# One row of the second MLP matrix in four loads on 16, 5, 11 and 3 DMA engines

## The chip, the cores and the metric

The kernel runs on one core of a Trainium2 chip: TensorE (PE), VectorE (DVE), ScalarE (ACT), GpSimd (POOL) and SyncE (SP), each with its own instruction stream, and 16 DMA engines that move data between HBM and the on-chip memory (128 partitions). The metric is the device time of one execution in microseconds, as the median of several runs. Before the change it is 364.54 us (3 runs, 364.46 to 364.63).

## The reference

One decode step: attention over the last 2048 positions of a key and value cache, an MLP on the same input rows, and a gate that mixes the two. All data are bfloat16.

```python
B, Sq, D = 8, 1, 576;  Hq, Hkv, Sk, Dh = 32, 16, 8192, 128      # MLP: F = 4608
g = sigmoid((x * gate_w).sum(-1))
q = (x @ wq) per head
a = softmax(q @ k[last 2048].T * Dh**-0.5) @ v[last 2048] @ wo
y = layernorm(x);  b = gelu(y @ w1 + b1) @ w2 + b2
out = g * a + (1 - g) * b
```

The cache parts that are read are 2 x 64 MB; `w2`, the second MLP matrix, has 4608 x 576 elements (5.3 MB).

## The kernel before

**How it is built.** `build_kernel` describes every operation as an `_Op` with its engine, the operations it waits for (`deps`), those it only has to stand behind (`after`), and a cost. `_Plan.schedule` (L62) runs a list schedule over these costs, which gives the order on each engine; `_Plan.emit` (L141) writes each engine's stream in that order, with semaphore waits for the `deps`. All loads are issued by SP on one hardware queue, and each one has the one before it in `after` (`last_dma`), so that their order is that in which the code makes them. A load raises its semaphore by 16 in all.

**Where the data lie.** All buffers are views of one tensor, `arena`; `req` reserves space, `over` lays a view over another one. `RAW` holds four slots of 32 KB a partition and a smaller fifth. `take_slot` goes round the four; a load into a slot waits for the slot's readers (`slot_free`). The views `sel` (L254) and `sel4` (L255) hold 0/1 matrices that PE reads once, near the start, in `sel_pe` (`o_selp`) and `h_pe` (`o_hp`).

**The stages.** At the start the query, the gate, and the hidden layer of the MLP are computed; `hT` holds the hidden layer transposed, 36 row groups of 128 rows (`FT = 36`). Then 16 units of attention (`NU`), each with a 4 MB K load and a 4 MB V load: VectorE transposes K, PE makes the scores, VectorE and ScalarE the softmax, PE the product with V. The list `stream` gives the order of the loads: K and V interleaved with K ahead, then at the end `("M", 0), ("W", 0), ("W", 1), ("M", 1)` (L594).

**The end.** `M` is a part of the second MLP matrix, `W` half of the attention's output matrix (`wo_chunk`, L832). Partition p of `w2` holds the rows 36 p to 36 p + 35, so that one "row" of the code is 576 elements (1152 B) in each of the 128 partitions. `M_CUTS` (L593) cuts the 36 into loads: `[24]` for the first part, `[8, 3, 1]` for the second. `m2_chunk` (L858) issues these loads, each with a semaphore of its own (`t0` to `t3`), and for each of them makes groups of matmuls: for every row two (288 columns each) that add `hT[:, row] x w2 row` into one PSUM bank. `AccGroup` (L570) is such a group; all groups of the end add into the same bank (`BK_ACC`), in the order of the list `o_m2`. When the last is done, VectorE and ScalarE copy the two halves out (L896 to L902), and SP stores the result (L903).

The lines that the change and the prediction speak of: the load of K and V (L618), the loads of the output matrix (L836), the loads of `w2` (L865), the matmuls of an `AccGroup` (L579), the product with V (L755, and its loop L188).

Of the kernel before, what the change touches and what calls it, by code (L numbers as in the profile page):

```python
# [6 lines left out]
BF = mybir.dt.bfloat16  # L7
F32 = mybir.dt.float32
ACTF = mybir.ActivationFunctionType
ALU = mybir.AluOpType  # L10
# [28 lines left out]
class _Plan:  # L39
# [10 lines left out]
    def add(self, eng, fn, deps=(), name=None, cost=0.1, after=(), prio=0):  # L50
        op = _Op(eng, fn, deps, name, cost, after=after, prio=prio)
        op.idx = len(self.all)
        self.all.append(op)
        return op

    def dma(self, eng, fn, semkey, nbytes, deps=(), name=None, after=(), prio=0):
        op = _Op(eng, fn, deps, name, self.DMA_ISSUE, after=after, is_dma=True, dma_sem=semkey, nbytes=nbytes, prio=prio)
        op.idx = len(self.all)
        self.all.append(op)
        return op  # L60
# [106 lines left out]
def _pst(t):  # L167
    return t.ap().ap[0][0]
# [23 lines left out]
        tile_size=(128, 128), tile_position=(0, 0)))  # L192


def build_kernel(nc, A_x, A_k_cache, A_v_cache, A_wq, A_wo, B_x, B_w1, B_b1, B_w2, B_b2, gate_w, out):
    B, Sq, D = A_x.shape
    _, Hkv, Sk, Dh = A_k_cache.shape
# [2 lines left out]
    W = min(4096, max(256, Sk // 4))  # L200
# [8 lines left out]
    ND = 4  # L209
    SE = 4 * W  # L210
    DE = 2 * SE
    FC, FT = 4, 36
# [12 lines left out]
    with ExitStack() as es:  # L225
        R = {}
        aoff = [0]

        def req(name, nelem, dt, align=64):
            sz = 2 if dt == BF else 4  # L230
            o = aoff[0] + ARENA_BASE
            o = (o + align - 1) // align * align - ARENA_BASE
            R[name] = (o, nelem, dt)
            aoff[0] = o + nelem * sz

        def over(name, base, off, nelem, dt):
            R[name] = (R[base][0] + off, nelem, dt)
            assert off + nelem * (2 if dt == BF else 4) <= R[base][1] * (2 if R[base][2] == BF else 4)
# [12 lines left out]
        req("idf8", 8, F32)  # L251
        req("dg", 16, F32)
        req("ones8", 128, F32)
        req("sel", 4 * 128, BF)  # L254
        req("sel4", 128, BF)  # L255
        req("cols", 16, F32)
        req("xT", 6 * 32, BF)
        req("yT", 6 * 32, BF)
# [17 lines left out]
        req("KT", 2 * SE // 2, BF)  # L276
        req("RAW", ND * DE + WOR * D, BF, 512)
        over("maskR", "PC", 0, 512, BF)
        over("out_sb", "PC", 1024, D, BF)
        over("KT2", "RAW", 2 * ND * DE, SE, BF)  # L280
        over("x_sb", "BD", 0, D, BF)
# [14 lines left out]
        arena = es.enter_context(nc.sbuf_tensor("arena", [128, (aoff[0] + 1) // 2], BF))  # L296
        AST = _pst(arena)
        arena_f = arena.bitcast(F32)

        def aoffs(name):  # L300
            return R[name][0] // 2
# [4 lines left out]
        def view(name, parts=128):  # L306
            o, n, dt = R[name]
            a = arena[0:parts, o // 2: o // 2 + (n * (2 if dt == BF else 4)) // 2]
            if dt == F32:
                a = a.bitcast(F32)  # L310
            return a
# [8 lines left out]
        sel = view("sel").rearrange("p (c m) -> p c m", c=4)  # L320
# [4 lines left out]
        sel4 = view("sel4", FC)  # L325
# [6 lines left out]
        hT = view("hT").rearrange("p (t b) -> p t b", b=32)  # L332
# [19 lines left out]
        def slot(s):  # L352
            return RAW[:, s * DE:min((s + 1) * DE, ND * DE + WOR * D)]
# [8 lines left out]
        def col(i, parts=128):  # L362
# [10 lines left out]
        OC = 64  # L373

        eng_sems = {e: es.enter_context(nc.semaphore("sem_" + e)) for e in ENGS}
        dma_keys = ["x", "g", "b", "b2", "wq", "w1", "out"] + ["s%d" % i for i in range(ND + 1)] + ["t%d" % i for i in range(5)]
        dma_sems = {k: es.enter_context(nc.semaphore("dma_" + k)) for k in dma_keys}

        P = _Plan()
        add, dma = P.add, P.dma  # L380
# [7 lines left out]
                   deps=[o_idf], name="r8", cost=0.2)  # L388
# [141 lines left out]
        o_selp = add("pe", sel_fn, deps=[o_qt, o_sel, o_xg], name="sel_pe", cost=0.9, prio=9)  # L530
# [20 lines left out]
        o_hp = add("pe", h_fn, deps=dw1 + db + [o_yT, o_xT, o_gcol, o_homg, o_sel4, o_obl], name="h_pe", cost=5.0)  # L551
# [10 lines left out]
        o_hT = add("dve", lambda e: e.transpose(view("hT"), bass.AP(arena, offset=aoffs("hb"), ap=[[AST, 128], [1, FT], [FT, 32]])), deps=[o_hf], name="hT", cost=1.3)  # L562
# [23 lines left out]
        NU = NG * NT  # L586
        stream, nk = [], 0
        for vi in range(NU):
# [1 line left out]
                stream.append(("K", nk))  # L590
                nk += 1
            stream.append(("V", vi))
        M_CUTS = [[24], [8, 3, 1]]  # L593
        stream += [("M", 0), ("W", 0), ("W", 1), ("M", 1)]  # L594

        last_dma = [d_w1r]
# [9 lines left out]
        def take_slot():  # L606
            n = n_slot[0]
            n_slot[0] += 1
            return (1, 2, 0, 3)[n % ND]
# [13 lines left out]
        def query(g):  # L623
            qb_done[g] = []
            for a in range(4):
                def fn(e, a=a):
                    dst = bass.AP(arena, offset=32 * a * AST + aoffs("qbd") + 640 * (g % 2) + 32 * a + 16, ap=[[AST, 32], [160, 4], [1, 16]])
                    src = bass.AP(arena, offset=32 * a * AST + aoffs("q4") + 32 * (NB_ * g + a // 2) + 16 * (a % 2), ap=[[AST, 32], [256, 4], [1, 16]])
                    return e.tensor_copy(dst, src)  # L629
                qb_done[g].append(add("pool", fn, deps=o_q4 + [o_qz, qk_unit.get(NT * (g - 1) - 1)], name="qr%d_%d" % (g, a), cost=0.3))  # L630
# [213 lines left out]
        o_m2, o_bias = [], []  # L844
# [10 lines left out]
        def bias(i):  # L855
            o_bias.append(AccGroup("m2_b", [(ob[:, 0:8], b2_sb), (ob[:, 8:16], b2_sb)], [d_b2, o_obl, o_obh], cost=0.6, after=[o_hp]).op)

        def m2_chunk(ci):  # L858
            s = take_slot()
            j = sum(sum(c) for c in M_CUTS[:ci])  # L860
            at = 0
            src = B_w2.rearrange("(p j) n -> p (j n)", j=FT)
            ops = []
            for n, jn in enumerate(M_CUTS[ci]):
                d = dma("sp", (lambda j=j, jn=jn, at=at: lambda e: e.dma_start(slot(s)[:, at * D:(at + jn) * D], src[:, j * D:(j + jn) * D]))(),  # L865
                        "t%d" % (sum(len(c) for c in M_CUTS[:ci]) + n), 128 * jn * D * 2, deps=slot_free[s] if n == 0 else [], name="d_w2_%d_%d" % (ci, n), after=last_dma[-1:])
                last_dma.append(d)
                mms = [(hT[:, j + k, 0:8], slot(s)[:, (at + k) * D:(at + k + 1) * D]) for k in range(jn)]
                for q in range(0, jn, 8):
                    ops.append(AccGroup("m2_%d_%d_%d" % (ci, n, q), mms[q:q + 8], [o_hT, d], cost=0.14 * min(8, jn - q), prio=-1 if ci == 0 else 0, after=o_m2[-1:]).op)  # L870
                    o_m2.append(ops[-1])
                j, at = j + jn, at + jn
            slot_free[s] = ops

        query(0)
        bias(0)
        for kind, i in stream:
            {"K": k_item, "V": v_item, "W": wo_chunk, "M": m2_chunk, "B": bias}[kind](i)

        seq = []  # L880
        for t in range(NU):
# [31 lines left out]
def bass_gated_mix__sliding_block_cached__mixer_channel_mlp__decode_kernel(  # L913
    nc: bass.Bass,
    A_x: bass.AP,
    A_k_cache: bass.AP,
    A_v_cache: bass.AP,
    A_wq: bass.AP,
    A_wo: bass.AP,
    B_x: bass.AP,  # L920
    B_w1: bass.AP,
    B_b1: bass.AP,
    B_w2: bass.AP,
    B_b2: bass.AP,
    gate_w: bass.AP,
    out: bass.AP,
):
    build_kernel(nc, A_x, A_k_cache, A_v_cache, A_wq, A_wo, B_x, B_w1, B_b1, B_w2, B_b2, gate_w, out)
# [28 lines left out]
```

## Time and profile before

| | |
|---|---|
| median of 3 runs | 364.54 us |
| span of the profiled execution, first to last instruction | 363.0 us |
| busy: PE, VectorE, ScalarE, GpSimd | 297.9, 231.4, 168.6, 22.9 us |
| DMA queue of the loads | 6092 packets, 154.30 MB |
| landing of the last three loads after their issue | 22.3 to 23.0 us |

The profile is of one execution. Its page gives busy time by engine, the span in 40 slices (a digit is the busy share in tenths), the DMA queues, and the chain of work that ended last. The timeline lists instructions as start, duration, engine, line, operation, target and source and count, with the idle time before them and what ended it in brackets. A window's row gives its length, the busy time of each engine with its number of instructions, then three columns: granted TensorE clock, mean busy share of the 16 DMA engines, and GB/s. PEld is PE's weight load, SPq the issue of a load by SP. A packet counts into the window in which it starts, so that a share can be a little over 1.

### The profile page before, as it was taken

How to read it: one execution, taken by the hardware profiler on the slowest of the kernel's cores; microseconds unless marked ns; L12 is line 12 of the kernel's file. 1: busy time of each engine (PE TensorE's matmuls, PEld its weight loads, DVE VectorE, ACT ScalarE, POOL GpSimd, SP SyncE). 2: the span in 40 equal slices, each digit the busy share in tenths (PEclk: the TensorE clock that was granted, in tenths of full speed). 3: DMA queues.
4: the chain of work that ended last, by engine and by line, in shares of the span. 5: the costliest groups of instructions: out<-in, count | busy, mean ns of one | idle time of the engine just before them, and what ended most of it. 6: DMA issues, size and time to landing. Idle time of an engine off the chain costs nothing.

```text
span 363.0 us, 4821 instructions
## 1 busy us (share of the span) xinstructions
PE 297.9 (82%) x1954; PEld 125.3 (35%) x1423; DVE 231.4 (64%) x166; ACT 168.6 (46%) x130; POOL 22.9 (6%) x52
## 2 busy tenths in 40 slices
PE   0456366999999979998897979997989698999875
PEld 0111000434252615242433417150615152436742
DVE  0452989576666694929385768566675949295720
ACT  1022106656647463663637373838374554656000
POOL 9032030000010000000100000000000000003000
PEclk9976598999999998999999989999999999999999
DMA  8999999999999999999999999999999999999996
GB/s 347 436 437 406 455 412 455 412 455 412 450 415 451 415 451 413 441 426 441 426 441 426 435 430 437 430 437 428 437 430 437 430 435 430 437 430 433 415 430 257
DMA packets 6102, 154.45 MB, mean 426 GB/s; under 512 B 694, under 2 KB 840, under 8 KB 1228
## 3 DMA queue, kind: packets, MB, share of 16 engines
q1 hardware_dynamic: 6092, 154.30, 98.8%
q8 instruction: 8, 0.13, 0.1%
q14 instruction: 2, 0.02, 0.0%
HBM read 154.29 MB, written 0.01 MB: 425 GB/s over the span
## 4 chain that ended last, share of the span: by engine, by line
DMA 56%; DVE 27%; PE 14%; issue 1%; ACT 1%; SPq 0%; POOL 0%
DMA arena<-in_A_k_cache_dram 47%; DVE arena L718 21%; PE ps L175 6%; DMA arena<-in_B_w_dram 6%; DMA arena<-in_A_x_dram 3%; DVE arena L668 2%; PE ps L188 2%; PE ps L755 2%; PE ps L732 2%; DVE arena L645 1%; PE ps L501 0%; PE ps L579 0%; DVE arena L557 0%; DVE arena L521 0%; ACT arena L536 0%
## 5 line engine op out<-in xcount | busy, mean ns | idle before, releaser
L718 DVE STREAM_TRANSPOSE arena<-arena 128x4096 f32<-128x4096 f32 (+1 forms) x34 | 141.7, 4175 | 21.9 <-DMA arena<-in_A_k_cache_dram 21.9
L674 ACT ACTIVATE arena<-arena 32x2048 bf16<-32x2048 bf16 x60 | 114.5, 1908 | 71.4 <-DVE arena L668 42.9
L175 PE MATMUL ps<-arena 128*128 128x512 bf16 (+3 forms) x531 | 136.1, 402 | 0.0
L188 PE MATMUL ps<-arena 128*128 x840 | 109.5, 277 | 7.3 <-issue 1.2
L188 PEld LDWEIGHTS ps<-arena 128*128 x840 | 81.4, 97 | 34.3 <-issue 19.0
L732 PE MATMUL ps<-arena 128*128 128x512 bf16 x128 | 51.4, 401 | 27.6 <-DVE arena L718 26.1
L645 DVE TENSOR_REDUCE arena<-ps 128x1 f32<-128x2048 f32 x16 | 36.7, 2291 | 53.8 <-PE ps L175 53.8
L732 PEld LDWEIGHTS ps<-arena 128*128 128x128 bf16 x128 | 12.5, 98 | 131.7 <-issue 75.3
L649 ACT ACTIVATE arena<-ps,arena 128x2048 bf16<-128x2048 f32 x16 | 40.7, 2543 | 0.5
L646 ACT ACTIVATE arena<-arena 128x1 f32<-128x1 f32 x16 | 3.2, 203 | 63.5 <-DVE arena L645 63.5
L755 PE MATMUL ps<-arena 128*128 128x256 bf16 x184 | 25.3, 272 | 1.1 <-DVE arena L663 1.1
L755 PEld LDWEIGHTS ps<-arena 128*128 128x128 bf16 x184 | 16.9, 99 | 18.8 <-issue 14.6
L668 DVE STREAM_TRANSPOSE arena<-arena 128x1024 f32<-128x1024 f32 x15 | 18.1, 1205 | 2.9 <-ACT arena L649 2.9
L579 PE MATMUL ps<-arena 128*8 128x288 bf16 (+1 forms) x140 | 9.6, 286 | 4.0 <-DMA arena<-in_A_wo_dram 3.3
L739 POOL MEMSET arena<- 128x4096 f32 x1 | 3.5, 3511 | 148.2 <-PE ps L175 148.2
L685 PE MATMUL ps<-arena 128*128 128x512 bf16 x16 | 6.5, 407 | 6.5 <-ACT arena L649 5.2
L629 POOL COPY arena<-arena 32x64 bf16<-32x64 bf16 x16 | 3.7, 229 | 123.3 <-PE ps L175 122.4
L901 ACT ACTIVATE arena<-ps 8x288 bf16<-8x288 f32 x1 | 0.4, 402 | 19.5 <-PE ps L579 19.5
L422 DVE COPY arena<-arena 8x128 bf16<-8x128 bf16 x2 | 0.5, 228 | 13.9 <-DMA arena<-in_A_x_dram 13.9
L579 PEld LDWEIGHTS ps<-arena 128*8 128x8 bf16 (+1 forms) x140 | 5.8, 86 | 9.9 <-DMA arena<-in_A_wo_dram 3.3
L900 DVE CAST arena<-ps 8x288 bf16<-8x288 f32 x1 | 0.4, 446 | 12.3 <-PE ps L579 12.3
L557 DVE TENSOR_TENSOR arena<-arena 128x1152 f32<-128x1152 f32 x1 | 1.4, 1358 | 9.7 <-ACT arena L555 9.7
(106 smaller groups left out, 94.0 us busy)
## 6 DMA issues: line engine op xcount, KB each, us to landing
arena<-in_A_k_cache_dram SPq DMA_DIRECT2D x16, 4096.0 KB, 28.7
arena<-in_A_v_cache_dram SPq DMA_DIRECT2D x16, 4096.0 KB, 25.5
arena<-in_B_w_dram SPq DMA_DIRECT2D x1, 4608.0 KB, 22.0
arena<-in_A_wo_dram SPq DMA_DIRECT2D x2, 2304.0 KB, 23.8
arena<-in_A_wq_dram SPq DMA_DIRECT2D x1, 4096.0 KB, 12.6
arena<-in_B_w_dram SPq DMA_DIRECT2D x1, 3456.0 KB, 24.1
arena<-in_B_w_dram SPq DMA_DIRECT2D x1, 1152.0 KB, 22.3
arena<-in_B_w_dram SPq DMA_DIRECT2D x1, 576.0 KB, 23.0
```

Source lines behind the costliest of these rows:

```text
L175: return e.add_instruction(mybir.InstMatmult(name=nc.get_next_instruction_name(), engine=mybir.EngineType.PE, ins=[e.lower_ap(rhs), e.lowe ...
L188: return e.add_instruction(mybir.InstMatmult(name=nc.get_next_instruction_name(), engine=mybir.EngineType.PE, ins=[rhs, lhsT], outs=[e.low ...
L579: ins = e.matmul(ps[32 * j:32 * j + 8, BK_ACC, 0:JN], lhsT, rhs[:, JN * j:JN * j + JN], start=False, stop=True, skip_group_check=True, til ...
L629: return e.tensor_copy(dst, src)
L645: mx = add("dve", lambda e: e.tensor_reduce(out=k(g, MX + x), in_=scores, axis=AXL.X, op=ALU.max), deps=[qk_unit[t]], name="mx%d" % t, cos ...
L649: ex = add("act", lambda e: e.activation(out=bass.AP(arena, offset=aoffs("P"), ap=[[AST, 128], [64, 32], [1, 2], [2, 32]]), in_=ps[:, 0:4, ...
L668: pc = add("dve", lambda e: e.transpose(view("PC").bitcast(F32), view("P").bitcast(F32)), deps=[ex] + (sp_done[t - 1][0] if t else [o_acc0 ...
L674: return e.activation(out=bass.AP(arena, offset=32 * a * AST + aoffs(home) + 64 * a, ap=[[AST, 32], [256, 32], [1, 64]]), in_=bass.AP(aren ...
L685: mm = e.matmul(*args, start=True, stop=False, skip_group_check=True) if n == 0 else held_matmul(nc, e, *args, start=True, stop=False, ski ...
L718: return e.transpose(bass.AP(arena_f, offset=foffs(base) + 2048 * h0, ap=[[AST // 2, 128], [1, 2048 * nh]]), bass.AP(arena_f, offset=foffs ...
L732: mm = e.matmul(*args, start=False, stop=True, skip_group_check=True) if rc == 0 else held_matmul(nc, e, *args, stop=True, skip=True)
L755: return e.matmul(dst, bass.AP(arena, offset=aoffs(home) + 256 * q + ee, ap=[[AST, 128], [2, 128]]), slot(s).rearrange("p (r k d) -> p r k ...
```

## The change

The last row (row 35) of each partition's part of `w2` leaves the 8-row load, which becomes one of 7 rows, and comes in four loads of its own, made by `row_part`. `X_PARTS` gives for each of them a number of DMA engines and of partitions on each: 16 x 1, 5 x 14, 11 x 3 and 3 x 3, which are 128 in all. The source of each load has the engines' number as its outermost dimension; `grouped_read` hands both patterns to the DMA instruction as they are. The four stand in `stream` behind the last V load and between the loads M0, W0, W1 and M1. They share one semaphore (`w2x`); the row's two matmuls (`m2_x`) wait for the last of the four and stand behind the second output-matrix group, ahead of the 7-row group. The row lies in a view `w2x` over the space of `sel` and `sel4`, and the first load waits for these views' readers.

```diff
+def grouped_read(nc, e, dst, src):
+    return e.add_instruction(mybir.InstDMACopy(
+        name=nc.get_next_instruction_name(), engine=mybir.EngineType.SP, queue="qSPDynamicHW", mode="Copy",
+        ins=e.lower_ap_dma(src), outs=e.lower_ap_dma(dst), oob_is_err=True, cce_op=ALU.bypass))
...
-        req("sel", 4 * 128, BF)
-        req("sel4", 128, BF)
+        req("selb", 5 * 128, BF)
...
+        over("sel", "selb", 0, 4 * 128, BF)
+        over("sel4", "selb", 1024, 128, BF)
+        over("w2x", "selb", 0, D, BF)
...
-        M_CUTS = [[24], [8, 3, 1]]
+        M_CUTS = [[24], [7, 3, 1]]
...
+            if ci == 1:
+                o_m2.append(AccGroup("m2_x", [(hT[:, FT - 1, 0:8], w2x)], [o_hT, d_w2x[-1]], cost=0.2, prio=-1, after=o_m2[-1:]).op)
...
+        w2x = view("w2x")
+        X_PARTS = [(16, 1), (5, 14), (11, 3), (3, 3)]
+        d_w2x = []
+
+        def row_part(i):
+            n, m = X_PARTS[i]
+            p0 = sum(a * b for a, b in X_PARTS[:i])
+            dst = bass.AP(arena, offset=p0 * AST + aoffs("w2x"), ap=[[AST, n * m], [1, 1], [1, D]])
+            src = B_w2.rearrange("(p j) n -> p (j n)", j=FT)[p0:p0 + n * m, (FT - 1) * D:FT * D].rearrange("(n m) c -> n m c", n=n)
+            d_w2x.append(dma("sp", lambda e: grouped_read(nc, e, dst, src), "w2x", n * m * D * 2, deps=[o_selp, o_hp] if i == 0 else [], name="d_w2x%d" % i, after=last_dma[-1:]))
+            last_dma.append(d_w2x[-1])
+
+        stream = stream[:2 * NU] + [("R", 0), ("M", 0), ("R", 1), ("W", 0), ("R", 2), ("W", 1), ("R", 3), ("M", 1)]
```

More of the change, by code (lines that the diff above doesn't have):

```diff
@@ L375, in build_kernel @@
         eng_sems = {e: es.enter_context(nc.semaphore("sem_" + e)) for e in ENGS}
-        dma_keys = ["x", "g", "b", "b2", "wq", "w1", "out"] + ["s%d" % i for i in range(ND + 1)] + ["t%d" % i for i in range(5)]
+        dma_keys = ["x", "g", "b", "b2", "wq", "w1", "w2x", "out"] + ["s%d" % i for i in range(ND + 1)] + ["t%d" % i for i in range(5)]
         dma_sems = {k: es.enter_context(nc.semaphore("dma_" + k)) for k in dma_keys}
@@ L873, in m2_chunk @@
             slot_free[s] = ops
+        w2x = view("w2x")
[8 more added lines that the diff above has]
+            last_dma.append(d_w2x[-1])
+        assert sum(a * b for a, b in X_PARTS) == 128
+        stream = stream[:2 * NU] + [("R", 0), ("M", 0), ("R", 1), ("W", 0), ("R", 2), ("W", 1), ("R", 3), ("M", 1)]
         query(0)
@@ L877, in build_kernel @@
         for kind, i in stream:
-            {"K": k_item, "V": v_item, "W": wo_chunk, "M": m2_chunk, "B": bias}[kind](i)
+            {"K": k_item, "V": v_item, "W": wo_chunk, "M": m2_chunk, "B": bias, "R": row_part}[kind](i)
         seq = []
```

## The prediction

> **What bounds the kernel now.** First the page: the engines' own lines, then the DMA queues and the chain that ended last.
>
> ```profile
> span 363.0 us, 4821 instructions
> ...
> DMA  8999999999999999999999999999999999999996
> ...
> q1 hardware_dynamic: 6092, 154.30, 98.8%
> q8 instruction: 8, 0.13, 0.1%
> q14 instruction: 2, 0.02, 0.0%
> HBM read 154.29 MB, written 0.01 MB: 425 GB/s over the span
> ...
> DMA 56%; DVE 27%; PE 14%; issue 1%; ACT 1%; SPq 0%; POOL 0%
> ```
>
> The DMA engines are full from the second slice to the last but one, and no other engine is. 154.3 MB have to come in; whatever PE, VectorE and ScalarE do between is hidden as long as the queue has work. A change of this kernel can therefore gain only by fewer bytes (there are none fewer here), by a faster rate, or at the two ends. So next the end: the last pieces of the chain in order of time, then the timeline of the same stretch.
>
> ```profile
> 337.01 0.02 issue
> 337.03 22.31 DMA arena<-in_B_w_dram
> 359.34 0.04 issue
> 359.38 1.71 PE ps L579 x24
> 361.10 0.02 issue
> 361.12 0.45 DVE arena L900
> ```
>
> ```profile
> 303.49 5.75 SPq L618 DMA_DIRECT2D arena<-in_A_v_cache_dram  x2
> 321.52 0.33 SPq L865 DMA_DIRECT2D arena<-in_B_w_dram  x1
> 329.90 0.81 SPq L836 DMA_DIRECT2D arena<-in_A_wo_dram  x2
> 337.03 1.28 SPq L865 DMA_DIRECT2D arena<-in_B_w_dram  x3
> 356.65 2.13 PE L579 MATMUL ps<-arena 128*8 128x288 bf16 x32 [1.46 <-DMA arena<-in_A_wo_dram]
> 359.38 0.83 PEld L579 LDWEIGHTS ps<-arena 128*8 128x8 bf16 x16 [0.93 <-DMA arena<-in_B_w_dram]
> 359.38 1.70 PE L579 MATMUL ps<-arena 128*8 128x288 bf16 x24 [0.61 <-DMA arena<-in_B_w_dram]
> 360.42 0.22 PEld L579 LDWEIGHTS ps<-arena 128*8 128x8 bf16 x6 [0.21 <-DMA arena<-in_B_w_dram]
> 360.79 0.09 PEld L579 LDWEIGHTS ps<-arena 128*8 128x8 bf16 x2 [0.15 <-DMA arena<-in_B_w_dram]
> 361.12 0.45 DVE L900 CAST arena<-ps 8x288 bf16<-8x288 f32 x1 [12.34 <-PE ps L579]
> 361.61 0.32 SPq L903 DMA_DIRECT2D out_dram<-arena  x1
> ```
>
> The last three loads (8, 3 and 1 rows of the second MLP matrix in each partition) are issued at 337.03 and wait some 22 us in the queue. PE gets the 8 rows at 359.38, the 3 at 360.42, the last one at 360.79; each time it was waiting. What follows 360.79 (two matmuls, the copy out, the store) takes 363.0 - 360.79 = 2.2 us and isn't touched. So the time is: the landing of the last row on the slowest DMA engine, and 2.2 us. How evenly the 16 engines reach that landing is told by windows over the last microseconds (the last two columns are the mean busy share of the 16 and GB/s):
>
> ```profile
> 40.00:320.00 280.00, 246.73 (x1482) 100.97 (x1056) 196.41 (x111) 150.11 (x107) 5.35 (x9) 0.97 1.00 433
> ...
> 356.00:358.00 2.00, 1.35 (x24) 1.01 (x25) 0.00 (x0) 0.00 (x0) 0.00 (x0) 1.00 0.99 416
> 358.00:358.50 0.50, 0.50 (x14) 0.36 (x8) 0.00 (x0) 0.00 (x0) 0.00 (x0) 1.00 0.94 387
> 358.50:359.00 0.50, 0.27 (x6) 0.00 (x0) 0.00 (x0) 0.00 (x0) 0.00 (x0) 1.00 0.84 332
> 359.00:359.25 0.25, 0.00 (x0) 0.00 (x0) 0.00 (x0) 0.00 (x0) 0.00 (x0) 1.00 0.67 263
> 359.25:359.50 0.25, 0.12 (x2) 0.09 (x4) 0.00 (x0) 0.00 (x0) 0.00 (x0) 1.00 0.69 272
> 359.50:359.75 0.25, 0.25 (x6) 0.18 (x4) 0.00 (x0) 0.00 (x0) 0.00 (x0) 1.00 0.56 226
> 359.75:360.00 0.25, 0.25 (x10) 0.18 (x5) 0.00 (x0) 0.00 (x0) 0.00 (x0) 1.00 0.48 180
> 360.00:360.25 0.25, 0.25 (x10) 0.18 (x4) 0.00 (x0) 0.00 (x0) 0.00 (x0) 1.00 0.44 157
> 360.25:360.50 0.25, 0.25 (x8) 0.09 (x4) 0.00 (x0) 0.00 (x0) 0.00 (x0) 1.00 0.10 32
> 360.50:361.00 0.50, 0.50 (x10) 0.18 (x7) 0.00 (x0) 0.00 (x0) 0.00 (x0) 1.00 0.00 0
> ```
>
> Times 16 the shares count engines still at work: 13 in the half microsecond before 359.0, then 11, 11, 9, 8 and 7, and under 2 after 360.25. So about half of the engines are done between 358.6 and 359.7 (the early ones), and the other half together between 360.1 and 360.45 (the late ones). The work left at 358.5 is 0.84 x 0.5 + (0.67 + 0.69 + 0.56 + 0.48 + 0.44 + 0.10) x 0.25 = 1.16 us of all engines; shared evenly it ends at 359.66 and not at 360.45. **0.8 us is the most that any sharing out can gain**: 0.2% of the time.
>
> Why half are late: the eight instruction fetches of the queue rows above, 0.13 MB / 8 = 16 KB each. At the 433 / 16 = 27 GB/s of one engine such a fetch is 0.6 us of that engine's time, and the table's 0.1% of 16 x 363 us, over 8, gives 0.7 (0.4 to 1.1 with its rounding). Eight fetches and eight late engines, none twice as late: I read it as one fetch on each. That the runs lie within 0.17 us of each other (364.46 to 364.63) says that the same thing happens every time.
>
> **The change, part by part.** *Row times.* From 359.38 to 360.42 the 3-row load came in, 24 descriptors' worth of rows on each engine: 1.04 / 24 = 43 ns a row; from 360.42 to 360.79 the 1-row load, 8 descriptors of 1152 B on each: 0.37 / 8 = 46 ns. By bytes at 433 GB/s these two would be 1.02 and 0.34, so another load behind a load costs 0.03 us at most.
>
> *Taken away*: the 8-row load becomes a 7-row load: 8 rows less on each engine, -8 x 43 = -0.34 us.
>
> *Added*: 16 rows at one on each of 16 engines, 70 at 14 on each of five, 33 at 3 on each of eleven, 9 at 3 on each of three. I take it that the sets are nested, the three among the five among the eleven. Then three engines get 21 rows (0.97 us), two get 18 (0.83), six get 4 (0.18) and five get 1 (0.05). Net: **+0.63, +0.49, -0.16 and -0.29 us**. The sum of rows is 128, as before; the mean over the 16 is +0.02.
>
> [...]
>
> *Which engines are late* is then what decides, and the views only count them. The packets' start times beneath the views can be followed from load to load on one engine; as far as I could follow them, the engine that carried every one-row load of the start is early, and so are most of those that shared these small loads, with a doubt about one; the late ones lie in the rest. I take it as likely, not as sure, that all five filled engines are early. Then the filled ones end at 358.6 to 359.7 plus 0.49 to 0.63, at 360.3 at the latest; the late ones at 360.1 to 360.45 less 0.16 or 0.29. If the latest lies among the six, the end is 360.29; if among the five with one row, it is 360.3 by the filled or the others. Ends: a gain of 0.15 to 0.30; with a filled engine at its bound and late rows slightly dearer, none. I take **-0.25**, near the large end, because five of the rest carry only one row, and only a latest engine among the six holds it to 0.16.
>
> *PE*: the row's two matmuls move ahead of the 8-row group, which has 14 instead of 16. 32 matmuls take 2.13 us, so two are 0.13; they fall into the 0.61 us for which PE waited before 359.38. If that load lands 0.25 earlier, 0.36 of the cover is left. Without it they would cost 0.13 there, and the last matmuls would still wait for the last row. The wait that they bring is for the fourth small load; behind it on PE are all remaining groups. That load follows the second output-matrix load on three engines, which by then carry 17 small rows (0.8 us) more. PE needs it at 356.65 + 2.13 = 358.8, when the load before it has been in for 2.1 us: covered, or 0 plus at most what exceeds 2.1.
>
> *SP*: four issues of about 0.4 us (0.33 alone, 0.81 for two). The first stands behind the last V load, issued by 309.24, and ahead of one that waits until 321.52; the second and the fourth lie in the waits before 329.90 and 337.03. Only the third holds anything up: the second output-matrix load is issued 0.4 us later and then has over 20 us of queue ahead. If that queue were empty, it would cost 0.4. The first carries a wait for two PE operations of the first 40 us. *The buffer* takes the place of selection matrices whose readers are those two; size and place of all else stay. Nothing.
>
> Sum: 363.0 - 0.25 = 362.75 for the span; the runs' median lies 1.54 above the profiled span, so 364.54 - 0.25 = **364.3 us**.
>
> **Rivals.** (1) *A filled engine is a late one.* Then it ends at 360.1 to 360.45 plus 0.49 to 0.63, which is 0.14 to 0.63 past the old end: about 364.95, slower. [...] For it: eight of sixteen are late, and no view shows which. Against it: what the packets' order let me follow.
>
> (2) *The filled engines take the end over, or the fetches fall elsewhere in the changed program.* The gain is given back: 364.5. PE's instructions are as many as before, so the fetches should fall as before.
>
> (3) *The sharing comes out almost even.* That takes late engines that lie just where the rows are fewest, and more than 0.29 us taken from each: 363.8, the bound of 0.8. No row count here takes off more than 0.34 in all, so it needs another gain, such as a steadier rate at the end (416 against 433 GB/s).
>
> (4) *The few-engine loads stall their engines*, at their start or because descriptors of 1152 B follow one another faster than they are fetched. Slack of the filled engines is 0.2 us at 360.3 against 360.45; at 0.3 us for each of the four on the first three engines it is +1.0: 365.5. Against it stands the 0.03 us of one load behind another. [...]
>
> **How the numbers follow.** Forecast 55%, its own range 364.2 to 364.5; (1) 15%, a fifth of it beyond 0.73 us by more than one such engine or a dearer row; (2) 9%; (3) 13%; (4) 8%. 0.2% is 0.73 us, about what a measurement of this kernel can tell from no change. Faster by more: (3), 13%. Slower by more: (4) and 3% of (1), 11%. Within: the rest, 76%. The range goes from 363.8, the bound, to 365.0, which holds most of (1); (4) and the far part of (1) stay out.
>
> **What would show it.** In the changed kernel's windows the shares should stay above 0.8 until past 359.25 and then fall within a shorter stretch, to 0 before 360.4. PE's last weight loads should begin near 360.55 instead of 360.79, and the whole tail after them stay 2.2 us. Two matmuls should stand alone ahead of the 7-row group, with no wait longer than the group's own had been. The queue rows should again have 8 and 2 fetches. Wrong is the forecast if one or two engines (shares of 0.06 or 0.12) work on after 360.5: then (1) or (4), and a rate in the windows around 345 to 351, where the filled engines work alone, tells these apart: (4) shows a dip there, (1) none.

## The result, and the profile after

| | before | after |
|---|---|---|
| median of 5 runs each | 364.54 us (364.43 to 364.68) | 366.88 us (366.42 to 367.70) |
| span of the profiled execution | 363.0 us | 365.6 us |
| ratio after to before | | 1.0068, 95% interval 1.0056 to 1.0080 |

The kernel became slower by 2.34 us, 0.64%; the forecast was 364.3, and its range ended at 365.0. (Two kernels below, `e7` and `e10`, had a second run in a slower state, of 386.45 and 532.64 us, which isn't counted.) The page of the changed kernel looks almost the same: still full DMA engines, the same bytes, the same 8 and 2 instruction fetches.

```profile
span 365.6 us, 4806 instructions
...
DMA  8999999999999999999999999999999999999996
...
q1 hardware_dynamic: 6255, 154.30, 98.8%
q8 instruction: 8, 0.13, 0.1%
q14 instruction: 2, 0.02, 0.0%
HBM read 154.29 MB, written 0.01 MB: 422 GB/s over the span
```

The same bytes came in at 422 GB/s instead of 425. The chain of waits of the changed kernel, in order of time, says from where on the time is late:

```profile
337.01 24.90 DMA arena<-in_B_w_dram
361.91 0.04 issue
361.96 1.03 PE ps L587 x14
362.98 0.01 issue
363.00 0.68 PE ps L587 x8
363.67 0.02 issue
363.70 0.45 DVE arena L925
```

The last part of the second MLP matrix is issued when it was (337.01, before 337.03). It lands 24.90 us later instead of 22.31, so the whole 2.58 us (361.96 against 359.38) is made between the two. From the copy out to the end nothing moved: 365.6 - 363.70 = 1.9, before 363.0 - 361.12 = 1.9. So next the windows of that stretch, first of the kernel before, then of the changed one (last three columns: granted TensorE clock, busy share of the DMA engines, GB/s).

```profile
336.00:345.00 9.00, 7.86 (x73) 6.70 (x71) 6.57 (x14) 0.30 (x1) 0.00 (x0) 1.00 0.96 412
345.00:351.00 6.00, 4.29 (x70) 2.71 (x59) 2.08 (x6) 0.00 (x0) 0.00 (x0) 1.00 1.01 430
351.00:358.00 7.00, 5.31 (x64) 2.55 (x58) 0.00 (x0) 0.00 (x0) 0.00 (x0) 1.00 0.98 419
```

```profile
330.00:336.00 6.00, 6.00 (x58) 5.40 (x57) 3.62 (x6) 2.98 (x4) 0.00 (x0) 1.00 0.99 427
336.00:345.00 9.00, 7.85 (x72) 6.69 (x71) 6.56 (x14) 0.30 (x1) 0.00 (x0) 1.00 0.99 359
345.00:351.00 6.00, 3.96 (x68) 2.72 (x59) 2.09 (x6) 0.00 (x0) 0.00 (x0) 1.00 0.95 371
351.00:358.00 7.00, 4.69 (x41) 2.24 (x35) 0.00 (x0) 0.00 (x0) 0.00 (x0) 0.76 1.02 392
...
361.00:362.00 1.00, 0.82 (x16) 0.41 (x12) 0.00 (x0) 0.00 (x0) 0.00 (x0) 1.00 0.82 326
362.00:363.00 1.00, 0.99 (x15) 0.51 (x16) 0.00 (x0) 0.00 (x0) 0.00 (x0) 1.00 0.50 187
```

Until 336 the rate is full. Then it falls by 53, 59 and 27 GB/s for 9, 6 and 7 us: 0.48 + 0.35 + 0.19 = 1.02 MB that have not come in by 358, and 1.02 MB at 425 GB/s are 2.4 us. **That is the lost time.** Two things are to be read in these rows. The share stays near 1 while the bytes fall: the engines are not idle, each packet takes longer. (By the packet records beneath the views, the packets of M0, of 27648 B, take 1253 ns in the median here; before it was 1025.) And the loss is far larger than the small loads themselves (0.15 MB in all): it lies in the big loads among which they stand. At the end the shares fall as before, half of the engines first (0.82, then 0.50), so no one or two engines were left behind.

The clock of 0.76 in 351 to 358 isn't what cost the time: PE waited 2.15 us for the first output-matrix load, as the timeline shows, and it still waited for the loads afterwards: 0.42 us for the second, 0.18 us for the last part.

```profile
353.48 3.80 PE L587 MATMUL ps<-arena 128*8 128x288 bf16 x32 [2.15 <-DMA arena<-in_A_wo_dram]
...
359.53 2.25 PE L587 MATMUL ps<-arena 128*8 128x288 bf16 x34 [0.42 <-DMA arena<-in_A_wo_dram]
361.96 1.70 PE L587 MATMUL ps<-arena 128*8 128x288 bf16 x22 [0.18 <-DMA arena<-in_B_w_dram]
```

### The profile page after: what moved, and what is told of

It reads as the page before. It is cut to its first block, busy times and chain, and to the rows that moved or that the text cites. A ratio compares the mean times of both kernels' runs of the same rounds, so it can differ in the third digit from the quotient of the medians.

```text
span 365.6 us, 4806 instructions
## 1 busy us (share of the span) xinstructions
PE 296.2 (81%) x1935; PEld 125.9 (34%) x1423; DVE 231.5 (63%) x166; ACT 168.6 (46%) x130; POOL 22.9 (6%) x52
## 4 chain that ended last, share of the span: by engine, by line
DMA 56%; DVE 27%; PE 14%; issue 1%; ACT 1%; SPq 0%; POOL 0%
DMA arena<-in_A_k_cache_dram 46%; DVE arena L726 20%; DMA arena<-in_B_w_dram 7%; PE ps L175 6%; DMA arena<-in_A_x_dram 3%; DVE arena L676 2%; PE ps L188 2%; PE ps L763 2%; PE ps L740 2%; DVE arena L653 1%; PE ps L587 0%; PE ps L509 0%; DVE arena L565 0%; DVE arena L529 0%; ACT arena L544 0%
## 5 line engine op out<-in xcount | busy, mean ns | idle before, releaser
L175 PE MATMUL ps<-arena 128*128 128x512 bf16 (+3 forms) x524 | 134.0, 397 | 12.1 <-DVE arena L726 9.2
L740 PE MATMUL ps<-arena 128*128 128x512 bf16 x122 | 48.4, 397 | 19.5 <-DVE arena L726 17.9
L587 PE MATMUL ps<-arena 128*8 128x288 bf16 (+1 forms) x140 | 11.4, 319 | 4.8 <-DMA arena<-in_A_wo_dram 2.6
L693 PE MATMUL ps<-arena 128*128 128x512 bf16 x11 | 4.4, 399 | 5.2 <-ACT arena L657 5.2
```

Source lines behind the costliest of these rows:

```text
L175: return e.add_instruction(mybir.InstMatmult(name=nc.get_next_instruction_name(), engine=mybir.EngineType.PE, ins=[e.lower_ap(rhs), e.lowe ...
L587: ins = e.matmul(ps[32 * j:32 * j + 8, BK_ACC, 0:JN], lhsT, rhs[:, JN * j:JN * j + JN], start=False, stop=True, skip_group_check=True, til ...
L693: mm = e.matmul(*args, start=True, stop=False, skip_group_check=True) if n == 0 else held_matmul(nc, e, *args, start=True, stop=False, ski ...
L740: mm = e.matmul(*args, start=False, stop=True, skip_group_check=True) if rc == 0 else held_matmul(nc, e, *args, stop=True, skip=True)
```

## The experiments

In the edits, R0 to R3 are the four small loads, M0, W0, W1, M1 the large ones around them; the edits are shortened to the lines that matter. Each kernel was compared with the kernel before on the same chip; that one's medians lay between 364.47 and 364.63, and the differences below are against the one that shared the chip. Where a kernel adds loads that nothing uses, it computes what the kernel before does. How many engines a load has is told as its pattern asks for it. For R0 to R3 the landing records in the trace of the changed kernel show it: when the rows come in, their semaphore is raised by 16, 5, 11 and 3 landings (at 336.0 to 337.6, 346.4 to 347.8, 351.7 to 353.5 and 358.8 to 359.4; one more for each of the last three comes near its issue). For the other small loads it is the design.

### Which of the four loads, and at which place

`e1_one16`: the row in one load, eight partitions on each of 16 engines.

```diff
-X_PARTS = [(16, 1), (5, 14), (11, 3), (3, 3)]
+X_PARTS = [(16, 8)]
+stream = stream[:2 * NU] + [("R", 0), ("M", 0), ("W", 0), ("W", 1), ("M", 1)]
```

> The row comes in one load on 16 engines, 8 rows on each, ahead of M0; the other three places are empty. Theory 1 (few-engine loads in the queue slow the stream behind them): M0 runs at 424 GB/s again in 338 to 344, and the time is 364.5 to 364.7. Theory 2 (any small-row load ahead of M0 does it, whatever its engines): M0 runs near 359 GB/s and the time is above 365.3. Theory 3 (a chance of how the engines stand to one another, not the loads): either, and profile and times need not agree.

`e2_four16`: four loads at the change's places, each on 16 engines with two partitions.

```diff
+X_PARTS = [(16, 2), (16, 2), (16, 2), (16, 2)]
```

> Four small loads at the same four places, each on 16 engines with 2 rows on each. Theory 1: full rate everywhere, 364.5 to 364.8. Theory 2: M0 near 359 GB/s, W0 and W1 slower as well, 366 or more. Theory 3: either.

`e3_late4` and `e4_r0late`: the change's own four loads at other places.

```diff
 # e3
+stream = stream[:2 * NU] + [("M", 0), ("W", 0), ("W", 1), ("R", 0), ("R", 1), ("R", 2), ("R", 3), ("M", 1)]
 # e4
+stream = stream[:2 * NU] + [("M", 0), ("R", 0), ("R", 1), ("W", 0), ("R", 2), ("W", 1), ("R", 3), ("M", 1)]
```

> The four loads of the change, all behind W1 and ahead of the 7-row load, so M0, W0 and W1 are as before. Theory 1 and 2: M0, W0 and W1 at full rate (424 GB/s in 338 to 344), whatever is slow is slow only after 357; 364.3 to 365.0. Theory 3: M0 may be slow again, 365.5 or more.

> As the change, but the 16-engine load stands behind M0, so that no small load is ahead of M0. Theory 1 (loads on few engines wait in the queue while M0 runs, as in the change): if waiting loads are enough, M0 stays near 359 GB/s; if they act only when they run, M0 is full and W0 and W1 are slow, 365.3 to 366.5. Theory 2: M0 at 424 GB/s, W0 and W1 slow, 365.3 to 366.5. Theory 3: either.

Measured: e1 365.09 (ratio 1.0017, 1.0004 to 1.0030), e2 365.32 (1.0018, 1.0008 to 1.0027), e3 365.50 (1.0026, 1.0016 to 1.0036), e4 365.76 (1.0027, 1.0017 to 1.0036). All lie between before and after: e1 and e2 between the times of theories 1 and 2, e3 above that of both though M0 has its full rate (419), e4 where both had it. The windows of e3, then of e4, tell more than their times:

```profile
345.00:353.00 8.00, 6.07 (x100) 4.13 (x91) 2.09 (x6) 0.00 (x0) 0.00 (x0) 1.00 1.02 433
353.00:357.00 4.00, 2.04 (x13) 0.14 (x3) 0.00 (x0) 0.00 (x0) 0.00 (x0) 1.00 0.97 355
```

```profile
338.00:344.00 6.00, 5.80 (x53) 5.09 (x54) 4.69 (x12) 0.30 (x1) 0.00 (x0) 1.00 0.98 421
345.00:350.00 5.00, 4.36 (x71) 2.77 (x60) 2.09 (x6) 0.00 (x0) 0.00 (x0) 1.00 1.00 373
351.00:353.00 2.00, 0.43 (x7) 0.32 (x9) 0.00 (x0) 0.00 (x0) 0.00 (x0) 0.97 0.91 332
353.00:357.00 4.00, 3.84 (x31) 1.81 (x25) 0.00 (x0) 0.00 (x0) 0.00 (x0) 0.59 1.01 434
```

**The dip goes where the small loads go.** With R0 to R3 behind W1 (e3) the rate is whole until 353. (By the packet records the small rows of e3 come in from 354.5 to 357.0, so most of its dip lies in their own stretch; packets of the 7-row load beside and behind them take up to 474 ns, most of them 305.) With R0 behind M0 (e4) M0 comes at 421 GB/s, where the change had 359 in its stretch, and the dip stands behind R0. So small loads slow what is queued behind them, and in e4 the last large load is whole again (434): the slowness isn't carried to the end every time. A stall of the filled engines alone (rival 4) would also have stayed where R1 to R3 are, but e1 and e2 fill no engine and still lost 0.51 and 0.74 us. e1 has the dip as well, though its row lies on all 128 partitions. This is its window where before had 424 and the change 359; the profiled run was one of its two long ones (366.25; eight of ten lay within 364.74 to 365.17), so the size of the dip isn't typical:

```profile
338.00:344.00 6.00, 5.94 (x54) 5.24 (x55) 4.58 (x11) 0.29 (x1) 0.00 (x0) 1.00 1.03 396
```

### One small load by itself, and thirteen

`e5_dum1`: the kernel before with one load added ahead of M0, 1152 B into each of the partitions 0 to 15, one on each of 16 engines. Nothing reads it. `e6_dum1_al`: the same with rows of 1024 B that begin at multiples of 512 B in the buffer. `e7_amp1`, `e8_amp1_al`: such a load (e7 as e5, e8 as e6) behind each of 13 V loads.

```diff
 # e5, on the kernel before
+n, m, E, p0, R0 = 16, 1, 576, 0, (FT - 1) * D
+dst = bass.AP(arena, offset=p0 * AST + aoffs("w2x"), ap=[[AST, n * m], [1, 1], [1, E]])
+stream = stream[:2 * NU] + [("R", 0)] + [("M", 0), ("W", 0), ("W", 1), ("M", 1)]
 # e6, e8
+n, m, E, p0, R0 = 16, 1, 512, 0, 32 * D
 # e7, e8
+p0 = 16 * (i % 8)
+stream = [x for it in stream[:2 * NU] for x in ([it, ("R", it[1])] if it[0] == "V" and 2 <= it[1] < NU - 1 else [it])] + [("M", 0), ("W", 0), ("W", 1), ("M", 1)]
```

> The kernel before with one more load of 16 rows of 1152 B, one on each engine, ahead of M0; nothing uses it, the computation is as before. Theory 2 (a small-row load slows the large load behind it): M0 well under 424 GB/s in 338 to 344, 365 or more. Theory 3 (chance alone): as before, 364.6 with its spread. By bytes the load costs 0.05 us.

> The same added load with 1024 B a row, source and target on multiples of 512 B; nothing uses it. Theory 2a (it is the rows' length and place, no multiples of 512 B, that slows what follows): M0 at 424 GB/s, 364.6. Theory 2b (any small load does it): M0 as slow as with 1152 B, 365 or more.

> The kernel before with 13 such loads of 16 rows of 1152 B, one behind each V load from the third to the last but one; nothing uses them. Theory 2: each slows the K load behind it by 0.5 to 1.5 us, 371 or more, rates of the K and V stage well under 433 GB/s. Theory 4 (only the weights' loads, with their own row distances, can be slowed): 433 GB/s in the K and V stage, 364.6 + 13 x 0.05 = 365.3.

> The same 13 loads with 1024 B rows on multiples of 512 B. Theory 2a: 365.2 and 433 GB/s. Theory 2b: as slow as the 1152 B rows. Theory 4: 365.2.

Measured: e5 368.81 (ratio 1.0115, 1.0098 to 1.0132), e6 366.60 (1.0039, 1.0014 to 1.0064), e7 377.61, e8 377.38 (1.0351, 1.0325 to 1.0376). **One load of 18 KB that nobody uses costs 4.2 us**, nearly twice the whole change. The windows of e5:

```profile
338.00:344.00 6.00, 5.96 (x54) 5.25 (x55) 4.57 (x11) 0.29 (x1) 0.00 (x0) 1.00 0.99 350
345.00:350.00 5.00, 3.14 (x55) 2.09 (x46) 1.64 (x5) 0.00 (x0) 0.00 (x0) 1.00 1.00 352
351.00:357.00 6.00, 3.01 (x34) 1.83 (x32) 0.00 (x0) 0.00 (x0) 0.00 (x0) 0.82 0.99 350
```

Every large load behind it comes at 350 to 352 GB/s with shares of 0.99 and 1.00, 17 to 21% below the kernel before, for some 20 us. The same windows of the kernel before:

```profile
338.00:344.00 6.00, 5.86 (x53) 5.17 (x54) 4.64 (x11) 0.30 (x1) 0.00 (x0) 1.00 0.98 424
345.00:350.00 5.00, 4.29 (x70) 2.71 (x59) 2.08 (x6) 0.00 (x0) 0.00 (x0) 1.00 1.04 446
351.00:357.00 6.00, 4.31 (x46) 1.81 (x41) 0.00 (x0) 0.00 (x0) 0.00 (x0) 1.00 0.99 422
```

That a row has 1152 B and isn't aligned is not the cause, as e8 shows. The runs of e6 fall into two heaps, four at 364.46 to 364.78 and six at 366.5 to 368.22, so that the same load may also cost nothing. In e7 slow and whole stretches alternate; by the packet records a slow one lasts from one small load to the next or the one after, and the 32 KB packets in it take 1353 to 1461 ns, nearly all of them alike, instead of 1213. The changed kernel shows the same (in the last two of these windows e5 has 362 and 359 GB/s):

```profile
345.00:347.00 2.00, 0.59 (x6) 0.28 (x3) 1.27 (x4) 0.00 (x0) 0.00 (x0) 1.00 0.99 320
347.00:350.00 3.00, 2.37 (x44) 1.69 (x39) 0.37 (x2) 0.00 (x0) 0.00 (x0) 1.00 0.97 412
...
353.00:357.00 4.00, 3.52 (x32) 2.13 (x32) 0.00 (x0) 0.00 (x0) 0.00 (x0) 0.58 0.95 369
```

While R1's rows come in (344.9 to 347.0 by the packet records) the rate is lowest; behind R1 the packets of W0 take 686 ns in the median, as before the change, and behind R2 those of W1 take some 766. In e5 both take some 836. So in this run each small load sets the rate of what follows anew, and the four cost less than R0 alone.

### Number of loads, few engines, the end, and half loads

`e12_cut4`: the kernel before with one load more, of the common kind: M0 in two loads of 4 and 20 rows on all partitions. `e11_amp5`: 13 unused loads as in e7, of 5 rows on 5 engines. `e9_tail4`: the change's four loads behind all others, their matmuls last. `e10_split`: 13 V loads cut into two, for partitions 0 to 63 and 64 to 127.

```diff
 # e12
+M_CUTS = [[4, 20], [8, 3, 1]]
 # e11
+n, m, E, p0, R0 = 5, 1, 576, 5 * i, (FT - 1) * D
 # e9
+stream = stream[:2 * NU] + [("M", 0), ("W", 0), ("W", 1), ("M", 1), ("R", 0), ("R", 1), ("R", 2), ("R", 3)]
 # e10
+cut = [(0, 64), (64, 128)] if which and 2 <= t < NU - 1 else [(0, 128)]
```

> The kernel before with M0 cut into 4 and 20 rows, so that a load of 4608 B pieces (590 KB) stands ahead of a large one in the tail. If any shorter load ahead does it: M0 under 400 GB/s, 365.5 or more. If only loads as small as the change's do: 424 GB/s and 364.5 to 364.8.

> As the 13 small loads of 1152 B rows, but 5 rows on 5 engines each; nothing uses them. If all 16 engines have to take a small load for the rate to fall: 433 GB/s, 364.6 to 365.3. If a small load on some engines is enough: slow stretches, 370 or more.

> The change with its four loads behind the last of all others, so that no large load stands behind a small one. Theory 2 (the small loads cost by slowing what stands behind them, and the sharing out itself is sound): all large loads at full rate (424 GB/s in 338 to 344), and the forecast's sum holds, 364.1 to 364.6. If the sharing out is wrong as well (a filled engine is a late one): 364.8 to 365.3 with full rates. Theory 3 (chance): slow stretches here too.

> The kernel before with 13 V loads cut in two of 64 partitions each: 13 more loads, all rows 32 KB. If the number of loads in the queue were the cause: slow K and V stretches as with the 13 small loads, 371 or more. Theory 2 (small loads): 433 GB/s in the K and V stage and 364.6 to 365.0.

Measured: e12 364.57 (ratio 1.0000, 0.9990 to 1.0009): another load of the common kind costs nothing by itself. e11 367.93 (1.0105, 1.0089 to 1.0120), with runs from 365.51 to 369.46; its profile is of the quickest, so what the others lost isn't located; a small load on five engines can cost, too, if less than was expected for that. e10 took 500.58 us: 37% more for 13 loads cut at partition 64, which no expectation had. Its profile is of the longer run, 532.64 us, so only the shape of its slices is read here. They are slices of the span in GB/s, then that of the same loads cut otherwise (`e16_split_even`, below):

```profile
GB/s 373 423 433 434 434 434 276 246 343 207 380 200 353 234 271 284 232 343 200 345 221 291 247 271 298 207 352 222 338 222 291 271 259 290 217 318 278 335 206 47
```

```profile
GB/s 347 432 441 406 459 408 459 408 459 408 454 412 455 412 455 410 449 419 448 419 448 415 446 419 444 423 441 424 441 426 441 426 435 430 433 433 429 423 420 267
```

From the seventh slice on e10 never comes back to its 434. A slice of 13 us mixes halves with uncut K loads; the lowest, 200 to 207, are a little under half of 434, and by the packet records the packets of the half loads take some 2500 ns instead of 1213.

e9 took 364.93 (1.0008, 0.9999 to 1.0017), the time expected if the sharing out is wrong as well. With nothing large behind the four loads the dip is gone, and what is left is the forecast's own mechanism. First its windows over the end, then the first of them of the kernel before, then a part of the timeline of e9:

```profile
359.00:360.25 1.25, 1.02 (x14) 0.55 (x14) 0.00 (x0) 0.00 (x0) 0.00 (x0) 1.00 0.73 231
360.25:360.50 0.25, 0.01 (x2) 0.01 (x4) 0.00 (x0) 0.00 (x0) 0.00 (x0) 1.00 0.10 32
360.50:360.75 0.25, 0.25 (x6) 0.17 (x6) 0.00 (x0) 0.00 (x0) 0.00 (x0) 1.00 0.00 0
```

```profile
359.00:360.25 1.25, 0.87 (x16) 0.64 (x16) 0.00 (x0) 0.00 (x0) 0.00 (x0) 1.00 0.57 219
```

```profile
359.04 0.71 PEld L587 LDWEIGHTS ps<-arena 128*8 128x8 bf16 x14 [0.66 <-DMA arena<-in_B_w_dram]
...
361.20 0.09 PEld L587 LDWEIGHTS ps<-arena 128*8 128x8 bf16 x2 [0.19 <-DMA arena<-in_B_w_dram]
```

More engines are at work (0.73 x 16 = 11.7 against 9.1), but each moves less: 231 / 11.7 = 19.8 GB/s against 219 / 9.1 = 24.0. The 7-row load is in at 359.04, 0.34 earlier than the 8-row load was, as forecast for a row less. The engines are empty when they were before (32 GB/s in 360.25 to 360.50 in both kernels, nothing after), and by the packet records the last packet ends at 360.36, before at 360.46. But PE waits for the small rows until 361.20, 0.84 us behind the last packet, where before it waited until 360.79, 0.33 behind it.

### Which side, and which partitions

Theory 5 of these expectations is that engines disturb each other where their rows cross on the partitions that they write. No view names a packet's engine, so which engine writes which partitions in a large load stays unknown here, and that rows spread by eights or by twos don't cross was an assumption.

`e13_dum_dst8`: e5's load with its 16 rows on the partitions 0, 8, ..., 120. `e14_dum_src8`: e5's load on partitions 0 to 15 as there, but read from the rows that belong to partitions 0, 8, ..., 120. `e15_amp_dst8`: 13 loads as in e7, each spread by eights. `e16_split_even`: e10's loads cut into the even and the odd partitions.

```diff
 # e13, e15
-ap=[[AST, n * m], [1, 1], [1, E]]
+ap=[[8 * AST, n * m], [1, 1], [1, E]]
 # e14
+src = B_w2.rearrange("(n p j) c -> n p (j c)", n=16, j=FT)[:, 0:1, R0:R0 + E]
 # e16
+bass.AP(arena, offset=aoffs("RAW") + s * DE + y * AST, ap=[[2 * AST, 64], [1, DE]])
```

> [...] Theory 5 (engines crossing on partitions): M0 at 424 GB/s, 364.5 to 364.8. Theory 2 (smallness alone): as with partitions 0 to 15, about 350 GB/s and 366.5 to 369.

> [...] Theory 5: as slow as the first one, 366 to 369. If it were the reading side: 364.5 to 364.8.

> [...] Theory 5: 433 GB/s in the K and V stage, 364.6 + 13 x 0.05 = 365.3. Theory 2: 375 or more, as with partitions that cross.

> [...] Theory 5: 433 GB/s, 364.6 to 365.0, where the halves took 516. If cutting a load is what costs: over 500 again.

Measured: e13 364.66 (ratio 1.0003, 0.9993 to 1.0012), e14 367.09 (1.0068, 1.0043 to 1.0093), e15 365.35 (1.0025, 1.0014 to 1.0036), e16 364.67 (1.0005, 0.9995 to 1.0016). Between e5 and e13 only the partitions written change, between e5 and e14 only the rows read; from e7 to e15 and from e10 to e16 the rows read move together with the partitions written. First e13, then e14 (the longest of its runs, 369.37), in the window where before had 424 and e5 350:

```profile
338.00:344.00 6.00, 5.81 (x53) 5.11 (x54) 4.68 (x12) 0.29 (x1) 0.00 (x0) 1.00 0.96 415
```

```profile
338.00:344.00 6.00, 5.83 (x53) 5.14 (x54) 4.67 (x12) 0.29 (x1) 0.00 (x0) 1.00 1.02 355
```

Then e7 and e15, over the long stretch in which before moved 433:

```profile
40.00:320.00 280.00, 236.83 (x1412) 95.37 (x998) 189.96 (x108) 142.48 (x102) 5.35 (x9) 0.97 1.01 414
```

```profile
40.00:320.00 280.00, 244.98 (x1478) 100.23 (x1052) 195.78 (x111) 150.15 (x107) 5.35 (x9) 0.99 1.00 433
```

**For these loads it is the partitions that are written.** The same number of rows, of the same bytes, costs 4.2 us on partitions 0 to 15 and 0.14 us on every eighth one. With the reading spread and the writing as in e5 it is slow still (2.6 us in the median). Thirteen of them cost 13 us on neighbouring partitions and 0.83 us spread: 0.06 for each, and a row takes 0.046. Cut into even and odd partitions, half loads cost nothing.

Two readings were open now. Either rows in one group of eight neighbouring partitions disturb each other (reading A), or it is another crowding of the rows, which those on every eighth partition don't have (reading B). `e17_dum_dst7` and `e18_dum_dst4` part them: e5's load on every seventh and on every fourth partition. By reading B both are harmless.

```diff
 # e17
+ap=[[7 * AST, n * m], [1, 1], [1, E]]
 # e18
+ap=[[4 * AST, n * m], [1, 1], [1, E]]
```

> The added load of 16 rows ahead of M0, on partitions 0, 7, 14 ... 105; nothing uses it. [...] Reading A: M0 well under 424 GB/s, 365.5 or more. Reading B: 424 GB/s and 364.5 to 364.8, as with every eighth partition.

> The same on partitions 0, 4, 8 ... 60; nothing uses it. By groups of eight neighbours two engines write in each of the first eight groups. Reading A: slow, 365.5 or more. [...]

Measured: e17 364.60 (ratio 1.0001, 0.9991 to 1.0010), e18 364.62 (1.0002, 0.9993 to 1.0012). In e18 each group of eight neighbours gets two rows, and nothing is slow; reading A falls. Its window of 338 to 344:

```profile
338.00:344.00 6.00, 5.74 (x52) 5.06 (x53) 4.75 (x12) 0.30 (x1) 0.00 (x0) 1.00 0.99 429
```

What the crowding of reading B is, no run shows, and the packet records don't show it either. In e5 the 16 rows start spread over 1.7 us and take 51 ns each, with at most three in flight at once; in the quick e13 it is the same, and in the quick e17 and e18 up to four are. So what the rows on neighbouring partitions change is seen only in the packets behind them.

## Why the prediction was wrong

- **What failed.** The row times: "another load behind a load costs 0.03 us at most". From it the sum prices the small loads by their own rows, and what they do to the large loads behind them stands at nothing. The 0.03 was measured on loads of all 128 partitions, and for these it holds (e12: nothing). It was carried over to loads of 16, 70, 33 and 9 neighbouring partitions, and there it is false by two orders: R0 alone is e5's load, 4.2 us by itself. (That the change with all four cost less, 2.34 us, goes with its windows: behind R1 it is back at 412 GB/s where e5 has 362.) The prediction counted how many rows each *DMA engine* gets and never asked where in the on-chip memory they are *written*.
- **Rival (4)** had the sign and came nearest (365.5), but its mechanism is wrong too. It put the stall on the filled engines, and asked for a dip at 345 to 351. The dip is there (371 GB/s against 430), but also at 336 to 345 behind R0, which fills no engine, and it is in packets of M0, which take 1253 ns in the median instead of 1025. Behind R1, which does fill engines, the packets of W0 take their 686 ns again, in the median. (Its 0.3 us for each load stands on no row, and no run shows the stall at a load's start or between descriptors that it names.) So the test that was to name (4) was passed by another cause: it asked for a dip and not for its place among the loads.
- **The sharing-out**, the forecast's own gain, is seen alone in e9. The shares at the end are evener, the row taken off gave its 0.34, and still e9 lies 0.34 above the kernel before (364.93 against 364.59; the interval just includes no difference). Two steps of the sum failed there. Rows at 43 to 46 ns are too cheap: each working engine moved 19.8 GB/s instead of 24.0 while the small rows came, so that the last packet ended 0.10 us earlier and not 0.25. And the sum took it that PE's last wait ends as long after the engines as before; it ended 0.84 us after the last packet instead of 0.33. Why it did, no run shows.
- **The bound of 0.8 us on any gain** was never reached by a kernel here: none is faster than the one before. (1), (2) and (3), which share out rows at their old price, decide nothing once the price is wrong.
- **Which engines are late**, and that each late one has carried an instruction fetch, was read from the counts and not tested, and so was that the five filled engines are early ones: no view names a packet's engine. Nor does any run show that the sets of engines are nested, from which the sum has 21, 18, 4 and 1 rows for an engine; the landing records show how many engines took each load (16, 5, 11 and 3) and not which. By the packet records of the kernel before each fetch took 0.88 to 0.97 us, a little more than the 0.6 to 0.7 that the prediction has.
- **What held**: the DMA engines bound the kernel, before and after; 1.9 us of copy and store follow the last matmul; 8 and 2 fetches; the two moved matmuls end no wait of their own (34 instead of 32 in the group at 359.53). Ahead of the fourth small load three engines carry, if the sets are nested, 1 + 14 + 3 = 18 small rows and not 17, which changes nothing. SP's issues were dearer than taken, 0.60 to 0.88 us and not 0.4, and cost nothing, as the queue was full (share 0.99 at 330 to 336).
- **Shown and not shown.** Shown: that the added loads make the slowness, that it follows their place, and that for the load of 16 rows it hangs on the partitions written and not on the number of loads, the row's alignment or the side read. Not shown: why loads on all partitions stay slow for up to 20 us behind one that is over in a fraction of a microsecond, and why in e6, e7 and e14 it strikes in some places or runs and not in others (of e14's ten runs two cost under 0.4 us and three over 4). Nor is it shown what reading B's crowding is: 16 rows side by side are slow (e5, 4.2 us) and 16 on every fourth, seventh or eighth partition are not (0.13 to 0.15 us), and no closer spacing of them was tried. And e1, whose 128 rows lie on all partitions, still lost 0.51 us and has the dip; that has no explanation here. So the partitions written aren't the whole cause.

## What to carry to other kernels

Look at a small load by the partitions it writes, not only by its bytes and engines: a few rows on neighbouring partitions can cost some ninety times their own time (4.2 us against 0.046), and they cost it in the big loads queued behind them. If a load must be partial, spread it over the partitions (16 rows on every fourth, seventh or eighth one and halves on every second one cost at most 0.15 us here) or put it last in the queue (0.34 us in e9, within its interval). That it reaches all partitions isn't enough, as e1 shows. A price for "one more load" read from full loads is no price for another shape; where a row of the profile shows full DMA shares with fewer bytes, look at what the packets write.

## What the runs showed that was not expected

- One load of 16 rows of 1152 B on partitions 0 to 15 lowered the rate of the loads behind it from 424 to 350 GB/s until the end, 4.2 us; on every fourth, seventh or eighth partition it cost 0.13 to 0.15 us, which is within the interval.
- A busy share of 1.00 doesn't mean the full rate: 433 GB/s and 352 GB/s both stand beside it.
- Thirteen loads cut at partition 64 made the kernel 37% longer; cut into even and odd partitions they made no difference.
